# Turning softmax weights through VectorE and DRAM instead of TensorE in a fused attention and feed-forward kernel

## The chip, the cores and the metric

One core of a Trainium2 chip. The metric is device time in microseconds (us), the median of three executions of the program.

## The reference

Four batches of 8 heads, 512 tokens x and 32 state rows, 64 channels a head. Attention runs both ways, and two feed-forward layers follow:

```
scores  = (x @ state.T) / 8 ;  a  = softmax over the 32 state rows ;  xread = a  @ state
scores2 = (state @ x.T) / 8 ;  a2 = softmax over the 512 tokens    ;  sread = a2 @ x
y   = concat([xread, sread]) laid out as [4 * 544 rows, 512]
h   = y @ moe_w_in  ; g = pos ? h : neg ? 0 : (h + 1)^2 / 4 ;  y = g @ moe_w_out
h   = y @ moe2_w_in ; g = max(h, 0) + log1p(exp(-|h|))      ; out = g @ moe2_w_out
```

The change is in `sread`: `a2`, the softmax over the tokens, has the tokens along the free axis when it is computed, and the product with x wants the tokens on the partitions.

## The kernel before

Weights are kept as a high and a low part, and a product is three TensorE passes (`mm3`). The first layer runs as windows: 16 for each batch of 512 tokens, 4 for all state rows together, then 16 more for the last batch; the second layer follows in the same form. A window i issues, in the order of the list `ORDER`, first `l1` (the product up into one PSUM bank of two), and `l2` (the product down, three windows behind) into four accumulators `acc0` to `acc3`. When a tile's 16 windows are through, `evac` copies the four accumulators into four tiles of the ring `xs` (four buffers, in turn; even ones by ScalarE, odd ones by VectorE) and SyncE stores them in DRAM (`xd`).

The attention of batches 2 to 4 (b = 1 to 3 in the code) is fitted between these products. It runs as steps of a generator: each window has two "hops", and a step's first half (TensorE) comes at one hop and its second half (ScalarE, VectorE) at the next one, so one step goes by with each window. `head()` turns x and makes the scores; `reads(True)` (batches 3 and 4) and `rest()` (batches 1 and 2) then go on, for the two groups g of 128 rows (4 heads by 32 state rows):

- `s_max`, `s_exp`, `s_norm` (L330 to L345): the softmax over the tokens, in the tile `e2[g]` (buffers `xT0` and `xT2`).
- `s_turn` (L347): for each group four 128x128 TensorE transposes (L350) into a PSUM bank; `s_keep` (L354): one ScalarE copy (L84) of that bank into `xT1` or `xT3`, which is `a2T[g]`.
- `s_read` (L362): 64 small matmuls (L370) that take `a2T[0]`, then `a2T[1]`, as their stationary side; `s_out` copies the result out.

The transposes of `n_` names belong to the other softmax, over 32 state rows; it uses VectorE's transpose (L325, L402), which turns each 32x32 block of a tile in its place. `HW[4]` is the window in which `rest()` of batch 2 begins; batch 1's begins at window 15. `load_x` (L176) loads the x of a batch, four DMAs of 256 KB. Nearly all DMAs are issued by SyncE's queue (SP), in order; a DMA there whose wait is not met holds up all behind it. Every DMA takes one of eight semaphores in turn and so also waits for the eighth DMA before it.

Of the kernel before, what the change touches and what calls it, by code (L numbers as in the profile page):

```python
# [9 lines left out]
F32 = mybir.dt.float32  # L10
# [8 lines left out]
def fused_kernel(ctx: ExitStack, tc: tile.TileContext, x, state, w1, w2, w3, w4, out):  # L19
# [6 lines left out]
    nc = tc.nc  # L26
    B, H, S, D = x.shape
    N = state.shape[2]
    DM, DF = w1.shape
    P = 128  # L30
    R = S // P
    NJ = H // 2
    NK = DM // P
    NF = DF // P
    NG = H * N // P
# [19 lines left out]
    base = ctx.enter_context(tc.tile_pool(name="base", bufs=1))  # L55
    dram = ctx.enter_context(tc.tile_pool(name="dram", bufs=1, space=bass.MemoryType.DRAM))
# [4 lines left out]
    at = at_cm.__enter__()  # L61
# [3 lines left out]
    def new(pool, shape, dt, tag, bufs=1):  # L65
        cnt[0] += 1
        return pool.tile(shape, dt, tag=tag, name=f"{tag}_{cnt[0]}", bufs=bufs)
# [11 lines left out]
    def at_bank():  # L79
        turn[0] ^= 1  # L80
        return side[:, turn[0] ^ 1, :]

    def copy(dst, src):
        nc.scalar.activation(dst, src, AF.Copy)  # L84
# [91 lines left out]
    def load_x(b, engs):  # L176

        t = new(at, [P, R * H * D], F32, f"x{b % 2}")
        src = x[b].rearrange("h (p r) d -> p h r d", r=R)
        if b == 0:  # L180
            t = t.rearrange("p (h r d) -> p h r d", h=H, r=R)
            xt[b] = t.rearrange("p h r d -> p r h d")
            for i in range(2):
                c = slice(i * NJ, (i + 1) * NJ)
                engs[i % len(engs)].dma_start(t[:, c], src[:, c])
        else:
            xt[b] = t.rearrange("p (r h d) -> p r h d", h=H, r=R)
            for r in range(R):
                engs[r % len(engs)].dma_start(xt[b][:, r], src[:, :, r])

    def warm(n, t=None):

        if t is None:
            t = bank("acc3", 1)
        for _ in range(n):
            nc.tensor.matmul(t[:, :P], ident, ident, start=True, stop=True)
# [51 lines left out]
    def place_state(st):  # L248
        ps = at_bank().rearrange("p (j c) -> p j c", j=NJ)
        for j in range(NJ):  # L250
            nc.tensor.transpose(ps[:, j, :], st[:, 2 * j : 2 * j + 2, :].rearrange("p e d -> p (e d)"), ident)
        nc.vector.tensor_copy(stT, ps)
# [26 lines left out]
    class Attn:  # L279
# [74 lines left out]
        def s_keep(self, g):  # L354
# [4 lines left out]
            self.a2T[g] = t.rearrange("p (r c) -> p r c", r=R)  # L359
            copy(t, self.ps[g])  # L360

        def s_read(self):  # L362

            xb = xt[self.b]
            self.ps["s"] = at_bank()[:, :P]
            for e in range(2):
                for r in range(R):
                    for j in range(NJ):
                        rows = slice(j * N, (j + 1) * N)
                        nc.tensor.matmul(  # L370
                            self.ps["s"][rows, e * D : (e + 1) * D],
                            self.a2T[e][:, r, rows],
                            xb[:, r, 2 * j + e, :],
                            start=(r == 0),
                            stop=(r == R - 1),
                        )
# [50 lines left out]
        def reads(self, s=True):  # L427


            def go(*fs):  # L430
                return lambda: [f() for f in fs]

            def both(f):
                return lambda: [f(g) for g in range(NG)]

            def when_s(*fs):
                return fs if s else ()

            yield None, go(lambda: self.blocks(0), *when_s(lambda: self.s_max(0)))
            yield None, go(  # L440
                *when_s(lambda: self.s_exp(0), lambda: self.s_max(1)), lambda: self.n_sub(0), lambda: self.blocks(1)
            )
            yield None, go(
                *when_s(lambda: self.s_exp(1), lambda: self.s_norm(0)), lambda: self.n_exp(0), lambda: self.n_sub(1)
            )
            yield None, go(*when_s(lambda: self.s_norm(1)), lambda: self.n_exp(1), lambda: self.n_norm(0))
            yield when_s(both(self.s_turn)), go(*when_s(both(self.s_keep)), lambda: self.n_norm(1))
            yield None, go(lambda: self.n_back(0), lambda: self.n_hi(0), lambda: self.n_lo(0))
            yield when_s(self.s_read), go(
                *when_s(self.s_out), lambda: self.n_back(1), lambda: self.n_hi(1), lambda: self.n_lo(1)  # L450
            )
# [34 lines left out]
        def rest(self):  # L486


            def both(f):
                return lambda: [f(g) for g in range(NG)]  # L490

            yield None, both(self.s_max)
            yield None, both(self.s_exp)
            yield None, both(self.s_norm)
            yield both(self.s_turn), both(self.s_keep)
            yield self.s_read, self.s_out


# [35 lines left out]
    for tl in [0, 1, 2, "s", 3]:  # L534
        n = NF // 4 if tl == "s" else NF
# [9 lines left out]
    for ti, us in enumerate(tiles2):  # L545
        start2.append(len(wins))
        n = NF // 4 if len(us) == 1 else NF
# [204 lines left out]
    def when(i, kind, fn):  # L752
        at_win.setdefault((i, kind), []).append(fn)
# [7 lines left out]


    TW = {(1, 6): 2, (2, 0): 3, (2, 4): 2, (2, 6): 2}
    HW = [3, 0, 4, 15, 17]
    A1 = [-3, 0, 2, 3, 6, 6, 7, 12]
    A2 = [-1, 2, 4, 4, 8, 10, 13, 15]
    pairs, early = [], []
# [19 lines left out]
    for n, (a, pair) in enumerate(pairs):  # L787
# [10 lines left out]
        n = 2 if a >= A0 else 1  # L798
# [32 lines left out]
    def plan_hops(i, *make):  # L831


        def start():
            def steps():
                for m in make:
                    for first, second in m():
                        for f in first if isinstance(first, tuple) else (first,):
                            if f is not None:
                                f()  # L840
                        yield
                        second()
                        yield

            gens.append(steps())

        when(i, "start", start)

    def attn(b):
        aT0[b] = Attn(b)  # L850
        return aT0[b]

    aT0 = {}
    when(HW[0], "pe", lambda: place_state(st))
    when(0, "pe", lambda: warm(W_[5]))
    when(1, "pe", lambda: warm(W_[6]))
    for b, i0, i1 in ((1, HW[1], HW[2]), (2, NF + 3, NF + 6), (3, 2 * NF - 1, 2 * NF + 1)):
        when(i0, "load", lambda b=b: load_x(b, [nc.sync]))
        plan_hops(i1, lambda b=b: attn(b).head(), lambda b=b: aT0[b].reads(b > 1))
    plan_hops(HW[4], lambda: aT0[1].rest())  # L860
    when(S0 - 3, "pe", place_x1s)
    plan_hops(HW[3], lambda: a0.rest())
    for ti in range(len(tiles2)):
# [136 lines left out]
```

## Time and profile before

| what | value |
|---|---|
| median of three timed executions | 735.79 us (735.77 to 736.36) |
| profiled execution: span from first to last instruction | 733.8 us |
| TensorE busy | 723.0 us, 99% |
| VectorE / ScalarE busy | 434.0 us, 59% / 450.4 us, 61% |
| 16 DMA engines, queue of SyncE | 20.8% |
| mean granted TensorE clock | 0.997 |

The page gives the span alone for the profiled execution; the median of the timed ones is 2.0 us longer than this span. "PE" is TensorE's matmuls, "PEld" its weight loads, "DVE" VectorE, "ACT" ScalarE, "POOL" GpSimd, "SPq" SyncE's queue of DMAs. In a timeline row the first two columns are the start and the duration in us, and a bracket at the end is the idle time just before it and who ended it. Many vector operations are issued before the one ahead has quite ended, so that starts lie closer than durations say.

### The profile page before, as it was taken

To read this page: it belongs to the slowest core of one execution; us is meant where nothing else is said; L and a number is where in the kernel's file an instruction comes from. 1 tells how busy PE (TensorE), PEld (TensorE's weight loads), DVE (VectorE), ACT (ScalarE), POOL (GpSimd) and SP (SyncE) were. 2 spreads that over 40 slices of the span, in tenths; PEclk is the share of its full clock that TensorE was granted. 3 is DMA by queue.
4 is the path that set the end of the run, shared out by engine and by line. 5 is a ranking of instruction groups with operands and counts; after the bars stand their busy time and mean duration, and the time that the engine had idled before them with its cause. 6 is when DMAs were issued, how large, how long until landed. Compare 5 with 4: busy or idle time off the path is not lost.

```text
span 733.8 us, 10265 instructions
## 1 busy us (share of the span) xinstructions
PE 723.0 (99%) x4102; PEld 582.8 (79%) x4102; DVE 434.0 (59%) x687; ACT 450.4 (61%) x742; POOL 17.1 (2%) x22
## 2 busy tenths in 40 slices
PE   8899999999999999999999999999999999999997
PEld 7577777778777887777888889888888888888886
DVE  5898874364485236668698846454464544554543
ACT  3787774564665436668688667555656556565553
POOL 0001200021000000000000000000000000000000
PEclk9999999999999999999999999999999999999999
DMA  9982007000101113334263011020001100010001
GB/s 334 345 290 82 0 1 171 4 1 1 58 1 59 59 42 132 130 119 168 75 210 132 1 58 59 0 72 1 0 1 63 53 1 0 1 58 0 1 1 58
DMA packets 36032, 52.11 MB, mean 71 GB/s; under 512 B 15568, under 2 KB 17424, under 8 KB 35984
## 3 DMA queue, kind: packets, MB, share of 16 engines
q1 hardware_dynamic: 35760, 51.26, 20.8%
q8 instruction: 32, 0.52, 0.3%
q10 hardware_dynamic: 224, 0.20, 0.1%
q14 instruction: 16, 0.13, 0.1%
HBM read 42.53 MB, written 8.91 MB: 70 GB/s over the span
## 4 chain that ended last, share of the span: by engine, by line
PE 93%; DMA 4%; DVE 1%; ACT 1%; issue 0%; SPq 0%; DVEq 0%
PE acc L561 17%; PE acc L563 16%; PE acc L562 16%; PE l L621 11%; PE l L563 8%; PE l L562 8%; PE l L561 8%; DMA wq<-in_moe_w_out_dram 3%; PE at L264 3%; PE l L608 2%; PE at L289 1%; DMA x<-in_x_dram 1%; PE at L370 1%; PE at L350 0%; DVE w L139 0%
## 5 line engine op out<-in xcount | busy, mean ns | idle before, releaser
L87 DVE TENSOR_TENSOR gtl<-tl,gth 128x512 fp32r<-128x512 f32 x64 | 44.3, 692 | 144.1 <-ACT gth L84 144.0
L719 ACT ACTIVATE ta<-l 128x512 f32<-128x512 f32 x68 | 40.7, 598 | 132.3 <-PE l L563 132.3
L561 PE MATMUL acc<-gth,wq 128*128 128x512 f32 x256 | 102.0, 398 | 0.0
L563 PE MATMUL acc<-gth,wq 128*128 128x512 f32 x256 | 99.9, 390 | 0.0
L562 PE MATMUL acc<-gtl,wq 128*128 128x512 f32 x256 | 99.8, 390 | 0.0
L87 DVE TENSOR_TENSOR gtl<-ta,gth 128x512 fp32r<-128x512 f32 x68 | 47.1, 693 | 54.7 <-ACT gth L84 54.7
L710 ACT ACTIVATE ta<-l 128x512 f32<-128x512 f32 x68 | 40.4, 594 | 39.7 <-PE l L621 15.8
L561 PE MATMUL acc<-wq,gth 128*128 128x512 f32 x152 | 59.3, 390 | 0.0
L563 PE MATMUL acc<-wq,gtl 128*128 128x512 f32 x152 | 59.2, 389 | 0.0
L562 PE MATMUL acc<-wq,gth 128*128 128x512 f32 x152 | 59.2, 389 | 0.0
L561 PEld LDWEIGHTS acc<-gth,wq 128*128 128x128 f32 x256 | 48.1, 188 | 12.3 <-issue 1.7
L563 PEld LDWEIGHTS acc<-gth,wq 128*128 128x128 f32 x256 | 48.1, 188 | 10.4
L562 PEld LDWEIGHTS acc<-gtl,wq 128*128 128x128 f32 x256 | 48.1, 188 | 9.4
L561 PE MATMUL acc<-wh,gth 128*128 128x512 f32 x136 | 53.0, 389 | 0.0
L562 PE MATMUL acc<-wl,gth 128*128 128x512 f32 x136 | 52.9, 389 | 0.0
L563 PE MATMUL acc<-wh,gtl 128*128 128x512 f32 x136 | 52.9, 389 | 0.0
L87 DVE TENSOR_TENSOR gl<-at,gh 128x512 fp32r<-128x512 f32 x23 | 15.9, 690 | 56.3 <-ACT gh L84 56.3
L87 DVE TENSOR_TENSOR tl<-tl,ta 128x512 f32<-128x512 f32 x68 | 47.0, 691 | 2.4
L729 DVE SCALAR_TENSOR_TENSOR tl<-l,tl 128x512 f32<-128x512 f32 x68 | 46.4, 682 | 0.0
L730 DVE SCALAR_TENSOR_TENSOR ta<-tb,ta 128x512 f32<-128x512 f32 x68 | 46.3, 680 | 0.0
L726 DVE SCALAR_TENSOR_TENSOR ta<-ta,l 128x512 f32<-128x512 f32 x68 | 46.1, 678 | 0.0
L84 ACT ACTIVATE gth<-ta 128x512 fp32r<-128x512 f32 x68 | 42.1, 619 | 5.2 <-DVE ta L726 5.2
(180 smaller groups left out, 1512.5 us busy)
## 6 DMA issues: line engine op xcount, KB each, us to landing
ws<-in_moe_w_in_dram SPq DMA_DIRECT2D x20, 512.0 KB, 4.6
ws<-in_moe_w_out_dram SPq DMA_DIRECT2D x20, 512.0 KB, 4.1
wq<-in_moe_w_in_dram SPq DMA_DIRECT2D x12, 512.0 KB, 8.7
wq<-in_moe_w_out_dram SPq DMA_DIRECT2D x12, 512.0 KB, 9.7
xd<-xs SPq DMA_DIRECT2D x16, 256.0 KB, 3.0
xs<-xd SPq DMA_DIRECT2D x16, 256.0 KB, 4.1
out_dram<-xs SPq DMA_DIRECT2D x15, 256.0 KB, 2.4
x<-in_x_dram SPq DMA_DIRECT2D x12, 256.0 KB, 4.6
```

The source lines that it names most:

```text
L84: nc.scalar.activation(dst, src, AF.Copy)
L87: eng.tensor_tensor(dst, a, b, op=ALU.subtract)
L264: nc.tensor.matmul(o(e)[j * N : (j + 1) * N, :], s_h, rhs(j)[rows], start=True, stop=True)
L561: nc.tensor.matmul(o, lh, rh, start=first, stop=False)
L562: nc.tensor.matmul(o, lh, rl, start=False, stop=False)
L563: nc.tensor.matmul(o, ll, rh, start=False, stop=last)
L621: nc.tensor.matmul(w.h, l[:, g, f], r[:, g, :], start=i == 0, stop=i == len(terms) - 1)
L710: nc.scalar.activation(w.a, w.hc, AF.Relu, bias=1.0)
L719: nc.scalar.activation(w.a, w.hc, AF.Abs)
L726: nc.vector.scalar_tensor_tensor(w.a, w.a, 1.0, w.hc, op0=ALU.min, op1=ALU.max)
L729: nc.vector.scalar_tensor_tensor(w.l, w.hc, 0.0, w.l, op0=ALU.max, op1=ALU.add)
L730: nc.vector.scalar_tensor_tensor(w.a, w.b, 1.0, w.a, op0=ALU.subtract, op1=ALU.subtract)
```

## The change

For batches 2 to 4, `s_turn` and `s_keep` go. In their place `s_block` follows `s_norm` on VectorE: it turns the 32x32 blocks of `e2[g]` into a tile z of the ring `xs`, SyncE stores z in a DRAM tile (128 rows of 2 KB), and four more DMAs read it back into `a2T[g]` with the blocks exchanged, each into 32 partitions, in runs of 32 numbers (128 bytes), 512 runs to a DMA. Two groups and three batches make 6 VectorE transposes, 6 stores and 24 reads. Batch 1 keeps its way. `rest()` of batch 2 begins one window earlier, with two steps left empty, so that `s_read` stays in window 21; in batches 3 and 4 the norm of group 1 and both blocks are in one step, and `s_read` is three steps on, as it was.

```diff
+        def s_block(self, g):
+
+            z = new(base, [P, S], F32, "xs", 4)
+            nc.vector.transpose(z, self.e2[g])
+            t = new(at, [P, S], F32, f"xT{2 * g + 1}")
+            self.a2T[g] = t.rearrange("p (r c) -> p r c", r=R)
+            zd = new(dram, [P, S], F32, f"zd{g}")
+            nc.sync.dma_start(zd, z)
+            zd = zd.rearrange("(j t) (r q n) -> q t r j n", j=NJ, r=R, q=NJ)
+            for q in range(NJ):
+                to = t[q * N : (q + 1) * N, :].rearrange("t (r j n) -> t r j n", r=R, j=NJ)
+                nc.sync.dma_start(to, zd[q])
+
...
-            yield None, go(*when_s(lambda: self.s_norm(1)), lambda: self.n_exp(1), lambda: self.n_norm(0))
-            yield when_s(both(self.s_turn)), go(*when_s(both(self.s_keep)), lambda: self.n_norm(1))
+            yield None, go(
+                *when_s(lambda: self.s_norm(1), both(self.s_block)), lambda: self.n_exp(1), lambda: self.n_norm(0)
+            )
+            yield None, go(lambda: self.n_norm(1))
...
-            yield None, both(self.s_norm)
-            yield both(self.s_turn), both(self.s_keep)
+            if self.b == 0:
+                yield None, both(self.s_norm)
+                yield both(self.s_turn), both(self.s_keep)
+            else:
+                yield None, lambda: [f(g) for g in range(NG) for f in (self.s_norm, self.s_block)]
+                yield None, lambda: None
+                yield None, lambda: None
...
-    HW = [3, 0, 4, 15, 17]
+    HW = [3, 0, 4, 15, 16]
```

SyncE's queue before, from the last weight loads of the first layer to the store of the second tile (`xd` are stores of a finished tile, `x` loads of a later batch):

```order
19 L116 DMA ws_627<-in_moe_w_out_dram 128x1024 x2
20 L695 DMA xd_6_78<-xs_1157 128x512
21 L695 DMA xd_6_78<-xs_1160 128x512
22 L695 DMA xd_6_78<-xs_1163 128x512
23 L695 DMA xd_6_78<-xs_1166 128x512
24 L189 DMA x_222_1201<-in_x_dram 128x8x64 x4
25 L189 DMA x_303_1782<-in_x_dram 128x8x64 x4
26 L695 DMA xd_7_79<-xs_1921 128x512
```

The same stretch now (`zd` is the DRAM tile of the bounce):

```order
19 L116 DMA ws_627<-in_moe_w_out_dram 128x1024 x2
20 L369 DMA zd_206_1105<-xs_1102 128x512
21 L373 DMA xT_205_1104<-zd_206_1105 32x16x32 x4
22 L369 DMA zd_209_1117<-xs_1114 128x512
23 L373 DMA xT_208_1116<-zd_209_1117 32x16x32 x4
24 L715 DMA xd_6_78<-xs_1181 128x512
25 L715 DMA xd_6_78<-xs_1184 128x512
26 L715 DMA xd_6_78<-xs_1187 128x512
27 L715 DMA xd_6_78<-xs_1190 128x512
28 L189 DMA x_228_1219<-in_x_dram 128x8x64 x4
29 L369 DMA zd_287_1618<-xs_1615 128x512
30 L373 DMA xT_286_1617<-zd_287_1618 32x16x32 x4
```

Both groups' stores and reads of batch 2 now stand ahead of the first tile's stores and of the loads of batch 3's x; the second group's store stands behind the first group's four reads.

VectorE before, in windows 18 and 19 (L343 to L345 are `s_norm`, L333 and L334 `s_max`, the two copies from `acc` the first tile's `evac`):

```order
130 L333 TENSOR_REDUCE nm_194_1050<-xT_115_607 128x1
131 L334 TENSOR_SCALAR nm_194_1050<-nm_194_1050 128x1
132 L333 TENSOR_REDUCE nm_195_1053<-xT_116_609 128x1
133 L334 TENSOR_SCALAR nm_195_1053<-nm_195_1053 128x1
134 L87 TENSOR_TENSOR gtl_1060<-ta_1005,gth_1059 128x512
135 L726 SCALAR_TENSOR_TENSOR ta_1056<-ta_1056,l_193_1024 128x512
136 L87 TENSOR_TENSOR gl_1114<-at_69,gh_1113 128x512
137 L87 TENSOR_TENSOR gtl_1103<-ta_1056,gth_1102 128x512
138 L693 COPY xs_1160<-acc_70_374 128x512
139 L693 COPY xs_1166<-acc_72_382 128x512
140 L726 SCALAR_TENSOR_TENSOR ta_1099<-ta_1099,l_199_1063 128x512
```

VectorE now, in the same windows (L365 is the new block transpose):

```order
135 L746 SCALAR_TENSOR_TENSOR ta_1060<-ta_1060,l_195_1030 128x512
...
138 L345 TENSOR_SCALAR xT_115_607<-xT_115_607,s_196_1056 128x512
139 L365 STREAM_TRANSPOSE xs_1102<-xT_115_607 128x512
...
142 L345 TENSOR_SCALAR xT_116_609<-xT_116_609,s_197_1058 128x512
143 L365 STREAM_TRANSPOSE xs_1114<-xT_116_609 128x512
144 L87 TENSOR_TENSOR gl_1138<-at_69,gh_1137 128x512
145 L87 TENSOR_TENSOR gtl_1127<-ta_1060,gth_1126 128x512
146 L713 COPY xs_1184<-acc_70_374 128x512
147 L713 COPY xs_1190<-acc_72_382 128x512
148 L746 SCALAR_TENSOR_TENSOR ta_1123<-ta_1123,l_201_1067 128x512
```

Batch 2's maximum (rows 130 to 133 before) has gone one window up and out of this stretch, its norms and block transposes have come ahead of the first tile's copies, and the second block tile (`xs_1114`) stands in the buffer that the copy of `acc3` (`xs_1190`) takes next.

## Rows read from the trace of the kernel before

**Rows 1.** The page: busy time, and the chain that ended last.

```profile
PE 723.0 (99%) x4102; PEld 582.8 (79%) x4102; DVE 434.0 (59%) x687; ACT 450.4 (61%) x742; POOL 17.1 (2%) x22
...
PE 93%; DMA 4%; DVE 1%; ACT 1%; issue 0%; SPq 0%; DVEq 0%
```

**Rows 2.** The chain, batch 4's turn and read: start us, us, what.

```profile
214.33 1.36 PE l L621 x6
215.70 0.87 PE at L350 x8
...
219.31 1.36 PE l L621 x6
...
223.38 1.36 PE l L621 x6
224.74 1.03 PE at L370 x64
```

**Rows 3.** The chain over the whole span: batches 2 and 3, and batch 3's x.

```profile
115.66 0.87 PE at L350 x8
...
121.44 1.03 PE at L370 x64
...
126.82 0.87 PE at L289 x8
...
171.75 1.03 PE at L370 x64
```

**Rows 4.** The line of VectorE's block transposes: duration ns min/median/max, first and last start.

```profile
L325 DVE STREAM_TRANSPOSE sa<-xT x6: 701/703/705, 59.8 to 205.2; 128x512 f32<-128x512 f32 x6
```

**Rows 5.** VectorE's timeline, the norm of group 1 in batch 3.

```profile
158.06 0.14 DVE L343 TENSOR_SCALAR s<-s 128x1 f32<-128x1 f32 x1
...
158.84 0.68 DVE L395 TENSOR_REDUCE sm<-sa 128x16 f32<-128x512 f32 x1
```

**Rows 6.** VectorE's timeline, the norm of group 1 in batch 4.

```profile
212.73 0.14 DVE L343 TENSOR_SCALAR s<-s 128x1 f32<-128x1 f32 x1
...
213.51 0.68 DVE L395 TENSOR_REDUCE sm<-sa 128x16 f32<-128x512 f32 x1
```

**Rows 7.** The page's DMA issues: count, KB each, median us from issue to landing.

```profile
xd<-xs SPq DMA_DIRECT2D x16, 256.0 KB, 3.0
...
xds<-xs SPq DMA_DIRECT2D x1, 256.0 KB, 2.0
```

**Rows 8.** The loads of batch 4's x by line, 122 to 126 us.

```profile
L189 SPq DMA_DIRECT2D x<-in_x_dram x4: 368/816/1824, 122.5 to 124.7; - x4
...
DMA to landing us min/median/max: 3.0/4.8/4.9
```

**Rows 9.** DMA queue, 122.5 to 130 us: packets, MB, share of 16 engines.

```profile
q1 hardware_dynamic: 4160, 1.05, 62.6%
```

**Rows 10.** The same, 298 to 300 us.

```profile
q1 hardware_dynamic: 144, 0.26, 34.8%
```

**Rows 11.** VectorE's timeline, windows 16 to 19.

```profile
99.23 0.69 DVE L87 TENSOR_TENSOR gl<-at,gh 128x512 fp32r<-128x512 f32 x1 [0.79 <-ACT gh L84]
...
102.60 0.68 DVE L333 TENSOR_REDUCE nm<-xT 128x1 f32<-128x512 f32 x1
...
104.17 0.68 DVE L87 TENSOR_TENSOR gtl<-ta,gth 128x512 fp32r<-128x512 f32 x1
104.77 0.68 DVE L726 SCALAR_TENSOR_TENSOR ta<-ta,l 128x512 f32<-128x512 f32 x1
...
110.69 1.28 DVE L693 COPY xs<-acc 128x512 f32<-128x512 f32 x2
```

**Rows 12.** TensorE's timeline, window 19.

```profile
110.22 1.10 PE L370 MATMUL at<-x,cv 128*32 128x64 f32 x64 [0.54 <-DVE gl L87]
...
113.45 0.39 PE L561 MATMUL acc<-gth,wq 128*128 128x512 f32 x1
```

**Rows 13.** The chain of the stretch 104 to 128 us, ahead of window 19.

```profile
105.89 1.40 ACT xT L339 x4
```

## The prediction

> **What bounds the kernel now.** I read three things in order. The page's busy times and chain first [rows 1]: TensorE is busy for 723.0 of 733.8 us and makes 93% of the chain; after the first weights have landed nothing else bounds it. So a change is worth what it takes from TensorE's row of work or what wait it puts there, and the time on VectorE, ScalarE and the DMA queue counts only where TensorE waits for it. Then the chain around the work that goes [rows 2, 3]. Last, the timelines of the engines that feed it [rows 5, 6, 11, 12], to learn when the new transfers can start and by when they must have landed. Everything behind 230 us is paced by TensorE, so what is gained or lost in windows 18 to 42 reaches the end undiminished.
>
> **What goes.** Each batch's turn is eight TensorE transposes, on the chain as one piece of 0.87 us [rows 2, 3]; there are three such pieces (115.66, one at 161.46 that is alike, 215.70). The cleaner measure is a window with the turn against the next without: 219.31 - 214.33 = 4.98 and 223.38 - 219.31 = 4.07 us [rows 2], so 0.9. Three of them: **2.7 us off TensorE**, which waited for nothing there. The six ScalarE copies that go too (`s_keep`) are worth nothing by themselves, since TensorE did not wait for them; they stood between the turn and the read, and the bounce takes their place.
>
> **What comes on VectorE.** Six block transposes of 703 ns [rows 4], 1.4 us a batch, in windows where VectorE is not on the chain; it is busy for 59% of the span and has gaps in each window. I cost them at nothing. If that cover failed it would be through the operation behind them that frees the product's PSUM bank one window later; 1.4 us against windows of 4.1 to 5 us leaves little, and I keep 0.4 us a batch as the upper end.
>
> **The bounce, from VectorE's tile to TensorE's read.** The trace has no such transfer, so I build it. Four legs run one after the other, because SyncE's queue is in order and the second group's store stands behind the first group's four reads: store 0, issue of reads 0, store 1, reads 1.
> - A store of 256 KB in 2 KB rows: 2.0 us alone, 3.0 us among its like [rows 7]. I take 2.0 for the first, since the queue is empty then, and 2.3 for the second, which finds packets of reads 0 ahead of it.
> - Issue: 368 ns for a load when nothing holds it up, 816 ns median when 1024 packets of 256 bytes each are ahead [rows 8]. I take four at 0.37, so 1.5 us; the upper end is four at 0.82, 3.3 us.
> - A packet: 4160 packets took 62.6% of 16 engines for 7.5 us [rows 9], 18 ns each, nearly all of 256 bytes; the 144 of 2 KB stores took 34.8% of 16 for 2 us [rows 10], 77 ns in the mean, with 16 tiny ones among them; without those some 86. A line through 18 and 86 gives 13 ns at 128 bytes. A read of 512 packets is 32 on each engine, 0.4 us, against 64 x 18 ns = 1.2 us in the load that landed in 3.0 us [rows 8]: so 2.3 us from issue to landing, and 3 x 0.37 + 2.3 = 3.4 us for reads 1. Upper end: 4.9 us for the last [rows 8] behind three issues of 0.82, 7.4 us.
> - Hand-overs between semaphore and queue: an allowance of 0.1 us each, four of them.
>
> Sum: 0.1 + 2.0 + 0.1 + 1.5 + 2.3 + 0.1 + 3.4 + 0.1 = 9.6 us. Lower end with both stores at 2.0: 9.3. Upper end with stores of 3.0: 3.0 + 3.3 + 3.0 + 7.4 = 16.7. These are far apart; the queue is empty at all three places and each read has half the packets of the loads, so I stay near the lower end and add 0.5 for a read pattern with one more dimension than any in the trace: **10.1 us**, with the second store landed 6.2 us after the start.
>
> **The time there is.** The tile is ready 0.78 us of norm and 0.70 us of transpose after the norm of group 1 begins; TensorE takes the second group's result 0.5 us into its read, and reaches it 0.9 us earlier than before.
> - Batch 4: ready at 212.73 + 0.78 + 0.70 = 214.2 [rows 6, 4]; due at 224.74 - 0.9 + 0.5 = 224.3 [rows 2]. Slack 10.1 us: just met.
> - Batch 3: ready at 158.06 + 1.48 = 159.5 [rows 5, 4]; due at 171.75 - 0.4 = 171.35 [rows 3]. 11.8 us: met by 1.7.
> - Batch 2: in window 18. Its maximum is gone from there (102.60 to 104.17, 1.57 us [rows 11]) into window 16, where 0.79 us of idle VectorE time takes half of it [rows 11]. So the operation at 104.77 comes some 0.7 us sooner, and the tile is ready near 104.1 + 0.6 + 1.5 = 106.2; due at 121.44 - 0.4 = 121.0 [rows 3]. 14.8 us: met.
>
> **What the bounce holds up.** Two things are behind it. First the ring `xs`: in window 19 the copy of `acc3` takes the buffer of batch 2's second block tile and so waits until store 1 has landed, at 106.2 + 6.2 = 112.4; with 0.7 us of copy it ends at 113.1, where it ended at 111.97 [rows 11]. TensorE wants `acc3` at 113.45 [rows 12], or 0.54 us sooner: its idle 0.54 before 110.22 was for VectorE's `gl` [rows 12], behind ScalarE's two exponentials of batch 2, 1.40 us [rows 13], which now run a window earlier. So the copy neither costs nor lets the whole 0.54 be gained: I book **0.3 us gained**, between 0.54 and a loss of 2.5 with store 1 at the upper ends (3.0 + 3.3 + 3.0 = 9.3, so 115.5 + 0.7 against 113.45). Second, the first tile's stores and the loads of batch 3's x: these wait for reads 1 (106.2 + 10.1 = 116.3), take some 7 us (122.5 to 129.6 for such a group [rows 8]), land near 123.5, and are wanted at 126.82 - 0.9 [rows 3]. Hidden, with 2.4 us to spare. Batch 4's x goes behind batch 3's bounce, which ends near 170, and is wanted near 180. Hidden.
>
> **The sum.** 2.7 + 0.3 - 0 = 3.0 us off the span, 733.8 to 730.8. The timed median stands 2.0 us above this span, and I carry that over: 735.8 - 3.0 = 732.8. Batch 4's slack is used up to the last tenth, so I take off 0.4 us for what a slightly longer bounce costs there and at `acc3`: **733.2 us**.
>
> A page of the Trainium skill speaks against this: DMA: Bandwidth & Descriptors (Specifications) says that transfers under 512 bytes at a time lose line rate, since the engine then reads, modifies and writes. The trace's 256-byte packets are under that size and took 18 ns where 2 KB ones took 86 [rows 9, 10], so at that size no doubling is seen; no row has 128 bytes. By the rule, estimated as twice 13 ns, both sets of reads take 1.7 us longer, and it would be the second rival below that comes true.
>
> **Rivals.**
> 1. The bounce takes 11.2 to 12.6 us, and the gain is eaten. Batch 4's read then waits 1.1 to 2.5 us, batch 3's up to 0.8, and `acc3` 0.1 to 1. At 11.7: 2.7 - 1.6 - 0.4 = 0.7 us gained, 735.1 us. For it: 816 ns is the median issue [rows 8], and four at 0.6 in either set already add 2 us. Against it: the loads that were held up had twice the packets and followed others.
> 2. The other side: short reads that cost far more than the line says, bounce near 13.5 us. Batch 4's read waits 3.4 us, batch 3's 1.7, `acc3` about 1.4: 6.5 - 2.7 = 3.8 us lost, **739.6 us**. It is slower by over 0.2% from a bounce of 12.6 us on. For it: no row has packets of 128 bytes, and the upper end of the legs is 16.7. Against it: the line through two sizes.
> 3. The change doesn't give what it says: TensorE saves its 2.7 us and waits them out elsewhere (the held-up loads of x, or VectorE late with 1.4 us more in its window); 735.8 us. For it: window 18 gets both norms and both transposes. Against it: 2.4 us of slack on x.
>
> **How the numbers follow.** A difference of 0.2%, 1.5 us, is about what a measurement of this kernel can tell from none: faster is under 734.3, slower over 737.3. Forecast 0.60 (bounce up to 11.2 us, which leaves 1.5 us or more), rival 1 0.20, rival 2 0.14, rival 3 0.06. So faster 0.60, same 0.26, slower 0.14. The forecast's own range is 732.5 (the whole 0.54 won, no wait) to 734.3; rival 1 and part of rival 2 stretch the upper end to 736.6.
>
> **What would show it.** No transposes at the turn, and windows 20, 29 and 40 at 4.1 us. The block tile to the last landing at 9.5 to 11 us, reads with 2 to 3 us from issue to landing, and issues under 0.5 us. At `s_read` no wait in batches 2 and 3 and at most 1 us in batch 4, by the DMA into `xT`. The copy of `acc3` ends near 113. Wrong it is if reads land later than 4 us after issue, if issues take 0.8 us, or if TensorE's wait at `s_read` in batch 4 is over 1.2 us.

## The result, and the profile after

The changed kernel takes 742.07 us in the median (741.03 to 743.24), the kernel before 736.08 beside it: a ratio of 1.0079 [1.0066, 1.0091], slower by 6 us. Forecast was 733.2, so the sign was wrong and 742.07 lies above the range. The profiled execution has a span of 739.9 us against 733.8.

The page, in the same lines as [rows 1] (engine, busy us, share of the span, instructions; then the chain that ended last, by engine):

```profile
PE 723.9 (98%) x4078; PEld 583.0 (79%) x4078; DVE 438.8 (59%) x693; ACT 447.4 (60%) x736; POOL 17.1 (2%) x22
...
PE 84%; DMA 7%; DVE 4%; ACT 2%; SPq 2%; issue 1%; DVEq 0%; ACTq 0%
```

TensorE has 24 instructions fewer and yet is busy for 0.9 us more, and its share of the chain fell from 93% to 84%: it now waits for others, and runs somewhere at a lower clock. The waits of TensorE between 90 and 260 us (engine, tile and line, waited for: us in all, times, longest) say for whom:

```profile
PE acc L581 <- DVE xs L713: 3.5, 1, 3.5
PE at L383 <- DMA xT<-zd: 2.4, 2, 1.6
PE at L383 <- DVE gl L87: 1.2, 1, 1.2
```

The code has moved 13 to 20 lines down: L383 is `s_read`, L581 to L583 are `mm3`, L641 is `l1`, L713 is VectorE's copy in `evac`, L369 and L373 are the bounce's store and reads. Before, the third of these waits was 0.54 us long [rows 12] and the other two were not there. Now the places. SyncE's queue in batch 2 and, behind the dots, batch 4 (start, us, line, what, how many):

```profile
109.24 0.33 SPq L369 DMA_DIRECT2D zd<-xs  x1
111.34 3.20 SPq L373 DMA_DIRECT2D xT<-zd  x4
114.64 0.58 SPq L369 DMA_DIRECT2D zd<-xs  x1
117.43 2.59 SPq L373 DMA_DIRECT2D xT<-zd  x4
...
219.94 0.32 SPq L369 DMA_DIRECT2D zd<-xs  x1
222.01 2.60 SPq L373 DMA_DIRECT2D xT<-zd  x4
224.71 0.57 SPq L369 DMA_DIRECT2D zd<-xs  x1
227.24 2.60 SPq L373 DMA_DIRECT2D xT<-zd  x4
```

Four legs in a row, as forecast, but four issues take 2.6 us where 1.5 was booked, and the first store of batch 2 starts at 109.24, not 106.2. Who was late is on ScalarE (the exponentials L339 of batch 2):

```profile
103.10 0.72 ACT L339 ACTIVATE xT<-xT,nm 128x512 f32<-128x512 f32 x1 [3.42 <-DVE xs L345]
...
103.88 0.72 ACT L339 ACTIVATE xT<-xT,nm 128x512 f32<-128x512 f32 x1
```

ScalarE stood idle for 3.42 us ahead of them, until VectorE's L345 of **batch 1** was through: the exponential writes its sums into the buffer `s2{g}`, batch 1's sums still lie there, and `rest()` of batch 2 now starts one window behind that of batch 1 instead of two. VectorE in the windows that follow (L365 is the block transpose; answers to [rows 11]):

```profile
108.50 0.71 DVE L365 STREAM_TRANSPOSE xs<-xT 128x512 f32<-128x512 f32 x1
...
110.01 0.71 DVE L365 STREAM_TRANSPOSE xs<-xT 128x512 f32<-128x512 f32 x1
...
111.81 0.68 DVE L713 COPY xs<-acc 128x512 f32<-128x512 f32 x1
117.47 0.69 DVE L713 COPY xs<-acc 128x512 f32<-128x512 f32 x1 [4.98 <-DMA zd<-xs]
```

The second copy, that of `acc3`, waits 4.98 us for the second store to leave the buffer it needs, and ends at 118.1 instead of 113.1. TensorE, in the places that answer to [rows 12] and [rows 2]:

```profile
111.35 1.10 PE L383 MATMUL at<-x,cv 128*32 128x64 f32 x64 [1.18 <-DVE gl L87]
...
118.22 0.50 PE L581 MATMUL acc<-gth,wq 128*128 128x512 f32 x1 [3.49 <-DVE xs L713]
...
119.06 1.05 PE L641 MATMUL l<-ahi,gh 128*128 128x512 f32 x2
...
177.81 0.65 PE L383 MATMUL at<-x,xT 128*32 128x64 f32 x32 [0.73 <-DMA xT<-zd]
...
231.77 0.65 PE L383 MATMUL at<-x,xT 128*32 128x64 f32 x32 [1.64 <-DMA xT<-zd]
```

The third row is a loss that nobody waits in: two matmuls take 1.05 us there, and pairs of the same line in the windows before and after it 0.61 to 0.73. The table of windows (stretch, length, then busy us and instructions of PE, PEld, DVE, ACT, POOL, then the granted clock, DMA share, GB/s) shows why:

```profile
115.00:117.00 2.00, 0.00 (x0) 0.00 (x0) 0.00 (x0) 0.00 (x0) 0.00 (x0) 1.00 0.62 173
117.00:119.00 2.00, 0.78 (x3) 0.67 (x4) 1.29 (x2) 0.21 (x1) 0.00 (x0) 0.99 0.10 16
119.00:121.00 2.00, 2.00 (x6) 1.55 (x5) 1.29 (x2) 0.42 (x1) 0.00 (x0) 0.50 0.57 91
121.00:123.00 2.00, 2.00 (x7) 1.57 (x7) 0.00 (x0) 1.11 (x2) 0.00 (x0) 0.66 1.01 342
```

Behind the idle stretch the granted clock is 0.50, the lower of its two levels (1.2 against 2.4 GHz), and back at 1.00 by 123 us. That costs 2 x 0.50 + 2 x 0.34 = 1.7 us of work at full clock.

The account, against the profile before: turns gone -2.7; longer wait for `gl` 1.18 - 0.54 = +0.6; `acc3` +3.5; low clock +1.7; waits at `s_read` +0.7 and +1.6. That is +5.4 of the 6.1 us between the spans. Another 0.5 arose by 42 us, ahead of everything changed (see the last section); 0.2 is not attributed.

### The profile page after: what moved, and what is told of

Read it like the earlier page. It is cut to its first block, busy times and chain, and to the rows that moved or that the text cites. A ratio compares the mean times of both kernels' runs of the same rounds, so it can differ in the third digit from the quotient of the medians.

```text
span 739.9 us, 10284 instructions
## 1 busy us (share of the span) xinstructions
PE 723.9 (98%) x4078; PEld 583.0 (79%) x4078; DVE 438.8 (59%) x693; ACT 447.4 (60%) x736; POOL 17.1 (2%) x22
## 4 chain that ended last, share of the span: by engine, by line
PE 84%; DMA 7%; DVE 4%; ACT 2%; SPq 2%; issue 1%; DVEq 0%; ACTq 0%
PE acc L581 15%; PE acc L583 15%; PE acc L582 15%; PE l L641 9%; PE l L583 8%; PE l L582 8%; PE l L581 8%; PE at L264 2%; PE l L628 2%; DMA wq<-in_moe_w_in_dram 2%; DMA zd<-xs 2%; DMA ws<-in_moe_w_in_dram 2%; SPq L373 1%; DMA wq<-in_moe_w_out_dram 1%; PE at L289 1%
## 5 line engine op out<-in xcount | busy, mean ns | idle before, releaser
L581 PE MATMUL acc<-gth,wq 128*128 128x512 f32 x256 | 102.1, 399 | 3.5 <-DVE xs L713 3.5
L583 PE MATMUL acc<-gth,wq 128*128 128x512 f32 x256 | 100.0, 391 | 0.0
L581 PEld LDWEIGHTS acc<-gth,wq 128*128 128x128 f32 x256 | 48.2, 188 | 16.3 <-DVE xs L713 3.9
L581 PE MATMUL acc<-wq,gth 128*128 128x512 f32 x152 | 59.3, 390 | 0.0
L583 PE MATMUL acc<-wq,gtl 128*128 128x512 f32 x152 | 59.2, 389 | 0.0
L583 PEld LDWEIGHTS acc<-gth,wq 128*128 128x128 f32 x256 | 48.2, 188 | 10.5
L581 PE MATMUL acc<-wh,gth 128*128 128x512 f32 x136 | 53.0, 389 | 0.0
L583 PE MATMUL acc<-wh,gtl 128*128 128x512 f32 x136 | 52.9, 389 | 0.0
```

Source lines behind the costliest of these rows:

```text
L581: nc.tensor.matmul(o, lh, rh, start=first, stop=False)
L583: nc.tensor.matmul(o, ll, rh, start=False, stop=last)
```

## The experiments

The theory after the result: three causes add up, (a) the shared sums, which make batch 2's tile late, (b) the bounce's legs one behind the other in SyncE's queue with dear issues, (c) the ring `xs`, through which (a) and (b) reach `acc3`. Rivals: the 128-byte reads fill the DMA engines, or TensorE would stand idle anyhow. All diffs are against the changed kernel.

**Batch 2 back to TensorE's turn.** It takes (a), (c) and batch 2's share of (b) away and leaves batches 3 and 4.

```diff
-            if self.b == 0:
+            if self.b <= 1:
...
-    HW = [3, 0, 4, 15, 16]
+    HW = [3, 0, 4, 15, 17]
```

> Batch 2 goes back to the TensorE turn (and begins in window 17 again); batches 3 and 4 keep the bounce. My theory puts 0.5 + 3.9 + 1.5 us of the loss on batch 2 (wait for gl, wait of acc3's copy on the ring xs, the low clock behind it), against 0.9 us saved by its missing turn, and 1.0 and 2.0 us on the reads of batches 3 and 4 against 0.9 us saved by each turn. So this kernel loses 5.0 us of the 6.0: 737.1 us, with no wait over 0.6 us in window 19 and the waits of batches 3 and 4 unchanged. The rival, that the six bounces cost in proportion (slow DMA traffic, each batch alike), expects a third of the 6 us back: 740 us.

Measured 737.38 us, 1.0029 [1.0012, 1.0045] of before. Its waits of TensorE, 90 to 260 us:

```profile
PE at L383 <- DMA xT<-zd: 2.4, 2, 1.9
PE at L383 <- DVE gl L87: 0.5, 1, 0.5
```

It is 1.6 us over before where the changed kernel is 6.0 over, so 4.4 us come in with batch 2, and the rival of equal shares (740 us) falls. The two later batches by themselves don't pay either: they save 2 x 0.9 = 1.8 us and wait 2.4. The last 1.0 of the 1.6 has a likely source in the profiled execution. One and the same matmul, far ahead of everything changed, starts here in the kernel before:

```profile
90.64 0.40 PE L561 MATMUL acc<-gth,wq 128*128 128x512 f32 x1
```

and in this run 0.9 us later:

```profile
91.58 0.40 PE L581 MATMUL acc<-gth,wq 128*128 128x512 f32 x1
```

Such a lateness comes with some executions and not with others of the same program (see the last section); that it lies behind the timed median too is not shown.

**A tile of its own for batch 2's blocks** takes away (c) alone: no copy shares a buffer with the stores.

```diff
-                t = new(base, [P, 1024], F32, "cv", 2)[:, :S]
+                t = new(base, [P, 1024], F32, "cv", 2)
+                t, spare[g] = t[:, :S], t[:, S:]
...
-            z = new(base, [P, S], F32, "xs", 4)
+            z = spare[g] if self.b == 1 else new(base, [P, S], F32, "xs", 4)
```

> Batch 2's two block tiles lie in free halves of two other tiles, so nothing in the ring xs waits for their stores; all else as in the change. My theory (the copy of acc3 waits for the second store through its buffer): the copy ends near 113.1 instead of 118.1, TensorE's 3.5 us idle and the low clock behind it go (5.4 us), but the loads of batch 3's x still wait for the reads at 122.3 and land near 130, where they are then due at 127.1, so 2 to 3 us come back as a wait there: 738.5 to 740.5 us. The rival, that VectorE is too full in windows 18 and 19 with the norms and block transposes and is late by itself, expects the copy as late as now and 742 us.

Measured 741.02 us, 1.0075 [1.006, 1.009]: a miss. The wait for `acc3` went, as expected, and the time did not. VectorE makes both copies of the first tile one behind the other from 111.34 us, so the rival that VectorE itself is late falls too. The waits of TensorE:

```profile
PE at L385 <- DMA xT<-zd: 2.9, 3, 1.5
PE at L290 <- DMA x<-in_x_dram: 2.5, 4, 0.7
PE at L385 <- DVE gl L87: 1.2, 1, 1.2
```

TensorE now comes early to batch 2's read and to batch 3's x, which stand behind the same late bounce in the queue; and the granted clock falls again, later (windows as above):

```profile
127.00:129.00 2.00, 0.85 (x4) 0.26 (x2) 0.00 (x0) 0.00 (x0) 0.00 (x0) 1.00 0.70 159
129.00:131.00 2.00, 0.66 (x2) 0.28 (x2) 0.00 (x0) 0.00 (x0) 0.00 (x0) 0.86 0.60 137
131.00:133.00 2.00, 1.99 (x8) 1.80 (x9) 0.00 (x0) 0.63 (x2) 0.00 (x0) 0.50 0.00 0
```

The ring was the place where the lateness showed, not its source. One wait taken from a late chain is found again at the next consumer.

**Sums of their own for batch 2** take away (a) alone.

```diff
-            self.s2[g] = new(at, [P, 1], F32, f"s2{g}")
+            self.s2[g] = new(at, [P, 1], F32, f"s2{g}" if self.b != 1 else f"s2b{g}")
```

> Batch 2's two row sums get buffers of their own, where the change lets them share those that batch 1's norm still reads in the same window. My theory: ScalarE's wait of 3.4 us before batch 2's exponentials goes, the block tile is ready near 106.7 instead of 109.2, the second store lands near 114.9 instead of 117.4, TensorE's wait for gl before batch 1's read goes (1.2 us), and its wait on acc3 falls from 3.5 to 1 to 2 us: 738 to 739.5 us. The rival, that the exponentials wait for VectorE's maximum itself and VectorE's queue sets the time, expects no change: 742 us.

Measured 738.47 us (737.76 to 741.35), 1.0045 [1.0028, 1.0061], so 2.7 us over before where the changed kernel is 6.0 over. (The profiled execution was the one of 741.35 us, so its span is not used. In it TensorE is 1.0 us later than in the changed kernel already at 91 us, 91.69 against 90.67 at the same L641, and its starts have to be read with that.) ScalarE's timeline, the first exponential of batch 2:

```profile
100.72 0.72 ACT L339 ACTIVATE xT<-xT,nm 128x512 f32<-128x512 f32 x1
```

TensorE's timeline, the matmul that needs `acc3`'s bank:

```profile
116.72 0.50 PE L581 MATMUL acc<-gth,wq 128*128 128x512 f32 x1 [2.17 <-DVE xs L713]
```

The exponential starts 2.4 us sooner, 3.4 with the late start taken off, and waits for nothing; the wait for `gl` is gone, and that for `acc3` fell from 3.49 to 2.17 (1 to 2 was expected). So the shared buffer is shown as a cause; what is left of the `acc3` wait is the bounce itself. Behind the shorter wait the clock falls as it did behind the longer one (windows as above):

```profile
117.00:119.00 2.00, 2.00 (x8) 1.53 (x8) 1.30 (x3) 0.63 (x1) 0.00 (x0) 0.70 0.57 91
119.00:121.00 2.00, 2.00 (x6) 1.61 (x5) 0.24 (x1) 0.89 (x2) 0.00 (x0) 0.50 0.79 238
```

With 0.95 from 121 to 123 us that is 2 x (0.30 + 0.50 + 0.05) = 1.7 us again.

**Both stores first, then all eight reads.** It changes the order in SyncE's queue and nothing else; the reads keep their form and number.

```diff
             nc.sync.dma_start(zd, z)
-            zd = zd.rearrange("(j t) (r q n) -> q t r j n", j=NJ, r=R, q=NJ)
-            for q in range(NJ):
+            self.zd[g] = zd, t
+
+        def s_fetch(self, g):
+            zd, t = self.zd[g]
+            zd = zd.rearrange("(j t) (r q n) -> q t r j n", j=NJ, r=R, q=NJ)
+            for q in range(NJ):
...
-                *when_s(lambda: self.s_norm(1), both(self.s_block)), lambda: self.n_exp(1), lambda: self.n_norm(0)
+                *when_s(lambda: self.s_norm(1), both(self.s_block), both(self.s_fetch)), lambda: self.n_exp(1), lambda: self.n_norm(0)
...
-                yield None, lambda: [f(g) for g in range(NG) for f in (self.s_norm, self.s_block)]
+                yield None, lambda: [f(g) for g in range(NG) for f in (self.s_norm, self.s_block)] + [self.s_fetch(g) for g in range(NG)]
```

> In SyncE's queue the second group's store goes ahead of the first group's four reads; same DMAs, same sizes. My theory (the serial legs of the queue make the bounce 12.4 us): in batch 2 the second store lands near 113 and acc3 does not wait, 5.4 us back; in batches 3 and 4 the last read lands 9.5 to 10 us after the tile is ready, and their waits of 1.0 and 2.0 us go: 733.7 us, faster than the kernel before. The rival, that reads in 128-byte runs fill the DMA engines, expects the reads to land no earlier in batches 3 and 4: 736.7 us with both waits there.

Measured 734.27 us, 0.9972 [0.9956, 0.9989]: faster than the kernel before. SyncE's queue in batch 2:

```profile
108.90 1.82 SPq L369 DMA_DIRECT2D zd<-xs  x2
110.98 6.03 SPq L377 DMA_DIRECT2D xT<-zd  x8
```

The waits of TensorE between 90 and 260 us:

```profile
PE at L387 <- DVE gl L87: 1.2, 1, 1.2
PE at L289 <- DMA x<-in_x_dram: 0.4, 1, 0.4
```

The last of the stores no longer waits behind four reads, nor do the last reads wait behind a store's landing. In batch 4 the last read is issued 6.8 us behind the first store's issue (213.78 to 220.6) instead of 9.3, and TensorE waits for nothing at `acc3` or for the reads. VectorE's row shows what the ring costs now, 0.37 us that TensorE does not feel:

```profile
112.51 0.69 DVE L717 COPY xs<-acc 128x512 f32<-128x512 f32 x1 [0.37 <-DMA zd<-xs]
```

The issue price is as before (634 ns in the median), so the same dear reads are harmless in another order, and the rival that reads of 128 bytes fill the DMA engines falls. This run also shows best what a turn is worth. Window 40, which took 4.98 us with the turn in it [rows 2], lies between these two matmuls:

```profile
213.71 1.07 PE L645 MATMUL l<-ahi,ws 128*128 128x512 f32 x4
...
217.79 0.39 PE L645 MATMUL l<-ahi,ws 128*128 128x512 f32 x1
```

That is 4.08 us, 0.9 less.

**Reads of one dimension fewer**, to learn why an issue costs 0.63 us.

```diff
-            zd = new(dram, [P, S], F32, f"zd{g}")
-            nc.sync.dma_start(zd, z)
+            zd = new(dram, [P, 2 * S], F32, f"zd{g}")
+            nc.sync.dma_start(zd[:, :S], z)
+            nc.sync.dma_start(zd[:, S:], z)
...
-                nc.sync.dma_start(to, zd[q])
+                nc.sync.dma_start(t[rows, :].rearrange("t (k n) -> t k n", n=N), zd[rows, :, 0, :])
```

> The reads keep their number, their 512 runs of 128 bytes each and their target, but take the runs from evenly spaced places of a DRAM tile of twice the width (one more store of 256 KB a group fills it; the exchange of the blocks is left out), so that the pattern has one dimension fewer on the DRAM side. It is for the issue price alone, 0.63 us in the change against 0.37 us that I took from the loads of x. Theory: the extra dimension makes an issue long: 0.37 us, so a group's four issues take 1.5 instead of 2.6 us. Rival: short runs or their number do it: 0.55 to 0.65 us as in the change. In both the extra stores add about a microsecond to each bounce, so the time of the whole, 739 to 743 us, says little.

The issues take 550 to 749 ns, 625 in the median: the dimension is not what is dear. (The time of its one execution, 747.02 us, has an added store in each group's bounce and says nothing else.)

**Reads of three other shapes**, on the same doubled stores.

```diff
+            n = {1: 64, 2: 32, 3: 512}[self.b]
+            src = zd.rearrange("p (k m n) -> p k m n", m=2, n=n)[:, :, 0, :]
+            to = t.rearrange("p (k n) -> p k n", n=n)
...
+                if self.b == 2:
+                    nc.sync.dma_start(to[:, q * 4 : (q + 1) * 4, :], src[:, q * 4 : (q + 1) * 4, :])
+                else:
+                    nc.sync.dma_start(to[rows], src[rows])
```

> Left out of the computation: the tile is stored in double width, the exchange of the token blocks is not made, and what the reads fetch back is not the turned tile; so only the issue price of the reads counts here, not the time. The store is that of e5 (two stores a group). The reads differ by batch: batch 2 fetches 32 partitions with 8 runs of 256 bytes each, batch 3 128 partitions with 4 runs of 128 bytes each, batch 4 one run of 2 KB for each of 32 rows. Three theories of the 0.63 us an issue takes (32 partitions, 16 runs of 128 bytes each). Run size (short runs are dear): batch 2 at 0.37 us as for the x loads, which have runs of 256 bytes, batch 3 at 0.63, batch 4 at about 0.33 as for a store. Number of runs per partition (16 against the x loads' 8): batch 2 at 0.37 to 0.45, batch 3 at 0.37, batch 4 at 0.33. Few target partitions (32 against the x loads' 128): batch 2 at 0.63, batch 3 at 0.37, batch 4 at 0.63. What tells most is batch 3: 0.63 by the first, 0.37 by the other two; batch 4 tells those apart.

The reads by line (duration of the issue in ns, min/median/max, first and last start), batch 2's second group, 32 partitions of 8 runs of 256 bytes:

```profile
L379 SPq DMA_DIRECT2D xT<-zd x4: 550/606/609, 119.1 to 121.0; - x4
```

Batch 3's first group, 128 partitions of 4 runs of 128 bytes:

```profile
L377 SPq DMA_DIRECT2D xT<-zd x4: 371/475/507, 169.5 to 171.0; - x4
```

Batch 4's two groups, one run of 2 KB in each of 32 rows:

```profile
L379 SPq DMA_DIRECT2D xT<-zd x8: 317/416/421, 223.3 to 228.5; - x8
```

None of the three theories holds. Runs of 256 bytes in 32 partitions are nearly as dear (0.61) as runs of 128 bytes (0.63), while runs of 128 bytes in 128 partitions cost 0.48 and one long run in each of 32 rows 0.42. Dear were only the reads with several runs in each of 32 partitions; neither the length nor the number of runs nor the 32 partitions alone does it. Why, stays open. A turn read into 128 partitions at a time was not tried, nor a second engine's queue. (The one execution took 740.95 us, which says as little as in the run before.)

**Combinations** of the edits above. Stores first with sums of their own, and then with the tile of its own too:

> Stores first as in the run before this one, and row sums of its own for batch 2. With the stores first 734.3 us were measured, and what was left there was a wait of 1.2 us for gl before batch 1's read and 0.4 us for batch 3's x. My theory puts the first on ScalarE held behind the shared sums: it goes, and the bounce is 2.4 us sooner, so x is in time as well: 732.7 to 733.3 us, ratio to the kernel before 0.996. The rival, that VectorE's norms and block transposes in window 18 make gl late by themselves, expects 734.3 us as with the stores first alone.

> As the run before, and batch 2's block tiles outside the ring xs as well. With the stores first the copy of acc3 waited 0.4 us on VectorE and TensorE not at all, so my theory expects no further gain: within 0.3 us of the run before. The rival, that the ring still costs something where nothing shows it, expects 0.5 us or more.

Measured 733.46 us, 0.9977 [0.9963, 0.999], a little above what was expected, and 733.9, 0.9979 [0.9965, 0.9994]. In the first TensorE has no wait at all between 90 and 260 us, so it would not have stood idle anyhow, and its page shows what the change had been meant to give:

```profile
span 731.0 us, 10285 instructions
...
PE 720.4 (99%) x4078; PEld 579.5 (79%) x4078; DVE 438.6 (60%) x693; ACT 447.7 (61%) x736; POOL 17.1 (2%) x22
```

The span is 2.8 us shorter than before, and 731.0 is 0.2 from the 730.8 of the forecast's sum. That the 2.8 is so near the 2.7 us booked for the three turns is in part luck: the wait of 0.54 us for `gl` [rows 12] went too, and smaller differences that were not attributed go the other way. Nor is TensorE's busy time, 2.6 us less than in [rows 1], a clean measure of the turns: from 10 to 20 us, ahead of all that was changed, TensorE was busy for 8.07 us here at a clock of 1.00, and for 9.10 us at 0.83 in the profile before. And the bounce's first store starts 2.6 us sooner than with the stores first alone (108.90):

```profile
106.31 1.82 SPq L369 DMA_DIRECT2D zd<-xs  x2
```

The tile adds nothing once the queue's order is right. The first combination was then run beside the kernel with the stores alone:

> The kernel with the stores first, once more, on the same chip as the next. In the profile of it TensorE has 1.2 us of wait for VectorE's gl behind batch 2's late exponentials and 0.4 for x. Theory: these waits lie on the path, so it takes 0.9 us more than the kernel that also has sums of its own. Rival: they are within what a measurement can tell, or are made up later, and the two differ by under 0.3 us. Both: 0.2 to 0.4% below the kernel before, 733.6 to 734.6 us where that takes 735.9.

> The kernel with the stores first and batch 2's sums in their own buffers, beside the last one. Theory: no wait of TensorE between 90 and 260 us, and 0.9 us less than the last one, so 732.9 to 733.5 where the kernel before takes 735.9. Rival: within 0.3 us of it.

Measured 734.07 us, 0.9975 [0.9964, 0.9987], and 733.56, 0.997 [0.9959, 0.9981]. The difference of 0.5 has the expected sign and lies between theory (0.9) and rival (under 0.3); the intervals overlap, so the times do not settle it. The profiles speak for the theory. In the first runs of the two kernels TensorE reaches the same L645 at 90.31 and 90.43 us, and the spans, 731.9 and 731.0, are 0.9 apart. In the second runs it comes there at 91.64 and 90.64, and of the 1.9 us between the spans 0.9 is left when this 1.0 is taken off. Both kernels are faster than the kernel before.

## Why the prediction was wrong

- **What bounds, and what goes: right.** A window without its turn takes 4.08 us where it took 4.98, so three turns are worth 2.7 us. VectorE's six transposes cost nothing: 0.71 us each, and with the order and the sums mended TensorE waits for nothing.
- **"The tile is ready near 104.1 + 0.6 + 1.5 = 106.2": failed.** It was 109.2. I had moved batch 2's maximum up a window and asked only whether VectorE had room there. The step brings its exponentials along, and I did not ask which buffers of batch 1 they take. With sums of its own the first store goes out 2.6 us sooner (108.90 to 106.31, both with the stores first), so the shared buffer accounts for 2.6 of the 3 us; the 0.5 us that this execution was late by 42 us covers the rest. Apart from the buffer the 106.2 was right. The same step booked a gain of 0.3 us on `gl`; it lost 0.6, and with sums of its own the wait for `gl` is gone.
- **"Four at 0.37, so 1.5 us": failed.** That was the lowest of the loads' issues in [rows 8], taken because the queue is empty; the median was 0.82. With an empty queue these reads took 0.63, four of them 2.6 us, in the second leg and again in the fourth. In batch 4 the bounce took 2.07 + 2.70 + 2.53 + 4.5 = 11.8 us (first store to last landing), and in batch 3 2.58 + 2.71 + 2.69 + 4.5 = 12.5, against 10.1. The reads' landing, 2.6 us in the median against 2.3, and the second store's leg, 2.5 to 2.8 against 2.4 with its hand-over, add the rest. The slack had been worked out as 10.1 and 11.8 us; being 1.7 and 0.7 over it gives the waits of 1.6 and 0.7. The deadlines were right, the size was not.
- **"Store 1 has landed at 112.4": failed,** by both steps above: 3.0 us from the late tile and 2.0 from dear issues and slower stores put the end of `acc3`'s copy at 118.1, where I had 113.1. I had bounded the loss there at 2.5 us (my own figures, 115.5 + 0.7 against 113.45, give 2.75), but from the same too early 106.2; it was 3.5. The own-tile run shows that this wait is only where the lateness surfaced. That the legs stand one behind the other I had seen, and took as given; the order was mine to change.
- **Not in the sum at all: the clock** behind the wait at `acc3`, 1.7 us. A wait was priced at its length.
- **The packets: right.** Four reads in batch 4, 227 to 232 us (packets, MB, share of 16 engines):

```profile
q1 hardware_dynamic: 2112, 0.26, 33.6%
```

  0.336 x 16 x 5 us / 2112 = 12.7 ns a packet, where the line through 256 bytes and 2 KB gave 13.
- **The rule against short transfers.** The Trainium skill, DMA: Bandwidth & Descriptors (Specifications), says that under 512 bytes a transfer loses line rate. This case's trace agrees that the rate falls: 12.7 ns for 128 bytes is 10 bytes a ns on an engine, 18 ns for 256 [rows 9] is 14, and 86 ns for 2 KB [rows 10] is 24. It does not bear out the doubling that the prediction made of the rule, 26 ns a packet.
- **The rivals.** The first had the bounce right: 11.2 to 12.6 us, with "four at 0.6" for its reason, waits of 1.1 to 2.5 us in batch 4 and up to 0.8 in batch 3; measured were 11.8 to 12.5, 1.64 and 0.73. Its 735.1 us failed at `acc3`, priced at 0.1 to 1 us; even with sums of its own the wait there was 2.17 us and the low clock came behind it. The second, 739.6 us, came nearer in time, by luck: its bounce of 13.5 us was dear by its packets, and its waits of 3.4 and 1.7 us at `s_read` are twice what was measured, while at `acc3` it had 1.4 and the runs show 3.5 + 1.7.
- **x of batch 3 is hidden** in the changed kernel, as forecast, but by luck: its loads are issued from 122.27 us, where the forecast had 116.3, and are in time only because TensorE is itself over 5 us late by then. When the `acc3` wait is removed, 2.5 us of waiting for x come to light.

## What to carry to other kernels

When a step is moved up, list every buffer that the steps behind it take and who still reads them, before asking whether the engines have room. In an in-order queue put all the stores ahead of the reads that wait on them: the same DMAs at the same price went from 6 us lost to 1.5 us gained by order alone. Price a DMA's issue from rows of its own shape where there are any, and not at the lowest row of another; and price a wait of TensorE at more than its length where rows show the clock falling behind such a wait, as it did here behind 2.2 and 3.5 us.

## What the runs showed of the hardware

- An issue on SyncE's queue with nothing ahead of it, and then the next one right behind: a store of 128 rows of 2 KB 0.32 and 0.43 us; a read of 16 runs of 128 bytes into each of 32 partitions 0.56 and 0.63; of 8 runs of 256 bytes into each of 32 partitions 0.55 and 0.61; of 4 runs of 128 bytes into each of 128 partitions 0.37 and 0.48; of one run of 2 KB into each of 32 rows 0.32 and 0.42.
- The low clock came behind TensorE's idle stretches at `acc3` (3.49 us in the changed kernel, 2.17 with sums of its own), and with the tile of its own behind a stretch from 127 to 131 us in which it was busy for 0.85 + 0.66 us, with its idle time in several waits. In all three it stood at 0.50 for a whole 2 us slice while TensorE was busy nearly throughout, and cost 1.7 us (with the tile of its own 0.86, 0.50 and 0.79 in the three slices from 129 to 135 us). Behind the wait of 1.64 us in batch 4 of the changed kernel the clock stayed at 1.00 (230 to 235 us).
- A low clock early in the program comes and goes without any change there. The table of windows, 10 to 20 us, in the first run of the kernel with the stores first:

```profile
10.00:20.00 10.00, 9.10 (x103) 6.40 (x101) 8.27 (x20) 4.27 (x9) 1.05 (x1) 0.83 1.04 398
```

The same in the second run of the same kernel:

```profile
10.00:20.00 10.00, 8.80 (x90) 5.94 (x89) 7.93 (x20) 3.47 (x6) 1.05 (x1) 0.66 1.04 398
```

  By 90 us TensorE is 1.3 us later in the second (91.64 against 90.31 at the same L645). The profiled executions of batch 2 back to TensorE's turn and of the sums of its own had 0.66 here too and were 0.9 and 1.0 us late. A second such stretch, 0.50 from 28 to 30 us, stood in the changed kernel and in the second run of the best combination, but not in the first, with spans of 731.2 and 731.0 us. So neither is the change's. Of the 0.5 us in the account above 0.3 stand at 40 us (40.51 against 40.23 for the same L289), and the rest comes by 42 us; how much of it is the clock's was not separated.
